# A long convolution with a gated layer behind it: late projections moved into the second half of a batch, taps read from SBUF, and an earlier start

## The chip, the cores and the metric

The kernel runs on one core of a Trainium2 chip. A core has a matrix engine (PE, with its weight loads listed apart as PEld), a vector engine (DVE), a scalar engine (ACT), GpSimd (POOL) and a sync engine (SP) that here issues every DMA. Each engine works through its own instructions in order; semaphores let one wait for another. The metric is the device time of the whole launch in microseconds (us); less is better. Before the change the median of three runs was 1005.45 us.

## The reference

`x` is (8, 6400, 128), eight sequences of 6400 positions with 128 channels, and `h` is (6400, 128). All is float32.

```python
def _attn_ref(x, h):                       # causal convolution along the sequence
    L = 2 * S
    Yf = np.fft.rfft(x, n=L, axis=1) * np.fft.rfft(h, n=L, axis=0)[None]
    return np.fft.irfft(Yf, n=L, axis=1)[:, :S, :]

def _moe_ref(x, w_val, conv_w, w_out):     # x is the convolution's result
    xp = np.concatenate([np.zeros((B, 4, D)), x], axis=1)
    gate_pre = sum(conv_w[k] * xp[:, k:k + S, :] for k in range(5))
    gate = 1 / (1 + np.exp(-gate_pre))
    return gate * (x @ w_val) @ w_out
```

So behind the convolution stand five taps per channel, a sigmoid, a product with a projection of the same data (128x128) and a second projection (128x128).

## The kernel before

The convolution is a transform of length 6400 = 100 x 64 written as matmuls against constant tables, done for one batch (one sequence) after another. Per batch there are four matmul stages.

- Stage 1 (`Forward`): sums and differences of the two halves of `x` are made by `sums` (both on POOL for batches 1 to 7, tile `sd`), then `half` multiplies them with the table `r1_sb` into a pair of PSUM banks; ACT copies the result into `gy`. There are 16 halves per batch, and `x` comes in 16 tiles of 128 x 512 numbers.
- Stage 2 (`Product`, 13 blocks `kb`): matmuls of `gy` with a streamed table (`m2`) into a PSUM pair, of which there are two. DVE multiplies the result twice with the spectrum of `h` (`mul_u` into `gy`, `mul_t` into the `h` tile), POOL adds (`add`, two instructions).
- Stage 3 (`s3_quads`, 16 of them): matmuls of `gy` with `r3_sb` into two single PSUM banks, one copied out by ACT, the other by DVE, into `dt`.
- Stage 4 (`Chunk.s4`, 13 chunks of positions: one HEAD chunk of 4 rows of 100, twelve of 5 rows): matmuls of `dt` with `m4_sb` into a single PSUM bank. There are four single banks, handed out in turn.

Then per chunk: `copies` (ACT: the data itself into `y`, the first tap, another tap into `p`), `taps` (three taps on DVE with scalar_tensor_tensor, and one addition on POOL), `project` (PE, two matmuls with the first weight), `sigm` (ACT), `gate` (DVE: projection in PSUM times the sigmoid in SBUF), `output` (PE, two matmuls with the second weight), `store` (ACT copies the result over `y`, SP writes it out). The taps of a chunk add onto cells that the chunk before it has touched too, so they follow each other.

The stages of successive batches overlap. A batch's time falls into two halves, which this text calls the first and the second half-stage:

- first half-stage: stage 3 of batch b, interleaved with stage 1 of batch b+1, 16 rounds;
- second half-stage: stage 4 of batch b, interleaved with stage 2 of batch b+1, 13 steps `s`. It is the loop over `s` at the end of the kernel. In step `s` PE gets the product of block s+1, the projection of chunk s-2, `s4` of chunk s, the output of chunk s-3; DVE gets `mul_u`, the taps of chunk s-1, `mul_t`, the gate of chunk s-2.

Five chunks (those from position row 35 to 59, the "late" ones) only have their data copied to `yl` tiles in the second half-stage. Their taps, and their and the HEAD chunk's projection, sigmoid, gate, output and store, are done in the next batch's first half-stage (`Gates.trail`). In the last batch nothing is late.

Nothing is scheduled by a planner: `_InOrder` keeps every engine's instructions in the order in which the code names them, so that order decides who stands behind whom. All instructions go through that helper, so the profile gives line 98 for nearly all; groups are told apart by tile names. A further piece is the start: `h` is transformed first, its spectrum is made and stored to DRAM, together with the products of batch 0, and `weights` (a generator, 22 DVE steps, that builds float32 weights from the 64-bit form) is advanced twice per block there.

## Time and profile before

| | |
|---|---|
| median of three runs | 1005.45 us (1003.25 to 1007.77) |
| the profiled execution, its own time | 1006.82 us |
| its span (first to last instruction) | 1005.0 us |
| PE busy | 940.5 us, 94% |
| DVE busy | 702.8 us, 70% |
| POOL busy | 544.5 us, 54% |
| ACT busy | 475.5 us, 47% |
| mean granted PE clock | 0.986 |
| one batch (as from 328.5 to 441.8 us) | 53.0 us first half-stage, 60.3 us second |

Rows of the timeline begin with start and duration, then engine, line, operation, output tile <- input tiles, shapes and a count of merged instructions; in square brackets stands how long the engine was idle ahead of it and whom it waited for. A float32 matmul of the program is listed as two. `pt<-dt,w_sb`, `pt<-yl,w_sb` and `pt<-gl,w_sb` are projections and outputs, `pt<-m_sb,dt` is stage 4, `pt<-gy,m` stage 2, `pt<-r_sb,gy` stage 3, `pt<-r_sb,sd` stage 1. On DVE, `gy<-pt,h` is `mul_u`, `h<-pt,h` is `mul_t`, `dt<-pt,dt` and `gl<-pt,gl` are gates, SCALAR_TENSOR_TENSOR are taps. Rows of the chain have start, duration and what the chain ran through.

### The profile page before, as it was taken

How to read it: one execution, taken by the hardware profiler on the slowest of the kernel's cores; microseconds unless marked ns; L12 is line 12 of the kernel's file. 1: busy time of each engine (PE TensorE's matmuls, PEld its weight loads, DVE VectorE, ACT ScalarE, POOL GpSimd, SP SyncE). 2: the span in 40 equal slices, each digit the busy share in tenths (PEclk: the TensorE clock that was granted, in tenths of full speed). 3: DMA queues.
4: the chain of work that ended last, by engine and by line, in shares of the span. 5: the costliest groups of instructions: out<-in, count | busy, mean ns of one | idle time of the engine just before them, and what ended most of it. 6: DMA issues, size and time to landing. Idle time of an engine off the chain costs nothing.

```text
span 1005.0 us, 46982 instructions
## 1 busy us (share of the span) xinstructions
PE 940.5 (94%) x21360; PEld 793.5 (79%) x21360; DVE 702.8 (70%) x939; ACT 475.5 (47%) x916; POOL 544.5 (54%) x551
## 2 busy tenths in 40 slices
PE   7897778999999999999999998999989999999987
PEld 7797778787978878887878778887887878786753
DVE  5499217977398747977398756977399755978366
ACT  4521434445543653546444554445544553534465
POOL 6467434785277744785177743784367752760032
PEclk9898999999999999999999999999999999999989
DMA  7783854756467545755467555665467554750012
GB/s 253 244 272 149 283 204 158 225 157 194 134 229 214 156 154 194 230 159 166 150 223 218 153 159 186 216 176 170 145 211 221 151 178 159 229 140 34 31 42 91
DMA packets 96838, 177.33 MB, mean 176 GB/s; under 512 B 43392, under 2 KB 49792, under 8 KB 96640
## 3 DMA queue, kind: packets, MB, share of 16 engines
q1 hardware_dynamic: 96640, 174.34, 55.6%
q8 instruction: 167, 2.74, 1.1%
q14 instruction: 31, 0.25, 0.1%
HBM read 141.55 MB, written 32.77 MB: 173 GB/s over the span
## 4 chain that ended last, share of the span: by engine, by line
PE 90%; issue 5%; DVE 3%; POOL 1%; ACT 1%; DMA 0%; POOLq 0%; DVEq 0%; ACTq 0%
PE pt L98 90%; DVE gl L98 1%; DVE dt L98 1%; POOL gl L98 1%; ACT dt L98 1%; DVE gy L98 0%; POOL dt L98 0%; DMA x<-hl 0%; DVE sd L98 0%; DVE m_sb L98 0%; POOLq L688 0%; ACT gl L98 0%; ACT yl L98 0%; ACT gy L98 0%; DVEq L98 0%
## 5 line engine op out<-in xcount | busy, mean ns | idle before, releaser
L98 PE MATMUL pt<-r_sb,gy 64*64 64x128 f32 (+1 forms) x8192 | 267.3, 273 | 20.3 <-issue 11.5
L98 PEld LDWEIGHTS pt<-r_sb,gy 64*64 64x64 f32 (+1 forms) x8192 | 235.8, 130 | 63.8 <-ACT gl L98 20.4
L98 POOL TENSOR_TENSOR sd<-x 128x256 f32<-128x256 f32 x236 | 197.4, 860 | 154.2 <-issue 124.2
L98 POOL TENSOR_TENSOR gy<-gy,h 128x512 f32<-128x512 f32 (+1 forms) x182 | 221.6, 1241 | 63.6 <-DVE h L98 27.7
L98 ACT COPY dt<-pt 128x512 f32<-128x512 f32 (+3 forms) x269 | 155.2, 581 | 193.9 <-PE pt L98 191.6
L98 PEld LDWEIGHTS pt<-m_sb,dt 128*64 128x64 f32 x4096 | 191.5, 137 | 35.3 <-issue 22.7
L98 PEld LDWEIGHTS pt<-gy,m 128*64 128x64 f32 x3008 | 179.1, 135 | 43.8 <-issue 23.6
L98 PE MATMUL pt<-gy,m 128*64 128x128 f32 x3008 | 193.3, 278 | 17.5 <-issue 12.0
L98 PE MATMUL pt<-m_sb,dt 128*64 128x100 f32 x4096 | 198.0, 250 | 2.9 <-DVE dt L98 2.4
L98 DVE COPY dt<-pt 128x512 f32<-128x512 f32 (+1 forms) x136 | 92.5, 680 | 132.1 <-PE pt L98 125.6
L98 PE MATMUL pt<-r_sb,sd 50*64 50x100 f32 x4608 | 143.2, 258 | 17.2 <-issue 11.2
L98 DVE TENSOR_TENSOR gy<-pt,h 128x1024 f32<-128x1024 f32 (+1 forms) x99 | 116.8, 1180 | 46.3 <-PE pt L98 46.3
L98 DVE SCALAR_TENSOR_TENSOR gl<-yl,w_sb,gl 128x500 f32<-128x500 f32 x147 | 130.6, 892 | 24.6 <-ACT gl L98 22.1
L98 PEld LDWEIGHTS pt<-r_sb,sd 50*64 50x64 f32 x4608 | 128.9, 142 | 22.2 <-issue 14.5
L98 DVE SCALAR_TENSOR_TENSOR dt<-pt,w_sb,dt 128x500 f32<-128x500 f32 (+7 forms) x216 | 132.9, 631 | 13.5 <-POOL dt L98 3.8
L98 ACT COPY gy<-pt 128x400 f32<-128x400 f32 x248 | 110.2, 496 | 41.2 <-PE pt L98 32.8
L98 ACT ACTIVATE dt<-pt,w_sb 128x500 f32<-128x500 f32 (+1 forms) x64 | 40.0, 625 | 170.2 <-PE pt L98 169.4
L98 PE MATMUL pt<-dt,w_sb 128*64 128x500 f32 (+2 forms) x480 | 116.0, 561 | 0.8 <-DVE dt L98 0.4
L98 POOL TENSOR_TENSOR dt<-dt,p 128x500 f32<-128x500 f32 (+1 forms) x64 | 66.4, 1038 | 82.5 <-DVE dt L98 58.0
L98 DVE TENSOR_TENSOR h<-pt,h 128x1024 f32<-128x1024 f32 (+1 forms) x91 | 107.3, 1179 | 2.3
L98 ACT COPY yl<-pt 128x500 f32<-128x500 f32 (+1 forms) x96 | 54.5, 568 | 83.9 <-PE pt L98 83.9
L98 DVE TENSOR_TENSOR gl<-pt,gl 128x500 f32<-128x500 f32 (+1 forms) x48 | 31.7, 661 | 54.5 <-PE pt L98 50.8
(40 smaller groups left out, 568.5 us busy)
## 6 DMA issues: line engine op xcount, KB each, us to landing
m<-m SPq DMA_DIRECT2D x90, 512.0 KB, 4.7
h<-hd SPq DMA_DIRECT2D x84, 512.0 KB, 3.9
x<-xl SPq DMA_DIRECT2D x118, 256.0 KB, 3.4
out<-dt SPq DMA_DIRECT2D x56, 250.0 KB, 5.8
out<-yl SPq DMA_DIRECT2D x40, 250.0 KB, 2.5
m_sb<-m SPq DMA_DIRECT2D x13, 375.0 KB, 4.5
hd<-h SPq DMA_DIRECT2D x8, 512.0 KB, 5.1
m_sb<-m SPq DMA_DIRECT2D x6, 512.0 KB, 6.5
```

Source lines behind the costliest of these rows:

```text
L98: return self._tc.keep_in_program_order(call(*args, **kwargs))
```

## The change

- The late chunks' and the HEAD chunk's `project`, `gate`, `output` and `store` are taken out of the next first half-stage and put into steps 0 to 4 of the next second half-stage (`pend`, `jobs`). The taps of the late chunks stay in the first half-stage, two per round, and so do two sigmoids; the rest of the sigmoids move.
- In every step, `output` and `store` now come one step after `project` for all chunks, with `output` at the head of a step and `project` at its end; a normal chunk is projected three steps after its stage 4 instead of two.
- On DVE the order within a step is `mul_u`, `mul_t`, the gates, then the taps.
- `copies` sets `self.p = self.y` for every chunk, so all taps on DVE read the copy in SBUF and no longer the PSUM bank.
- In the last batch both copies of a stage 3 quad are on ACT.
- Seven matmuls on a zeroed tile stand at the start of the program (`WARM`).
- The 22 weight steps move from the stage that makes `h`'s spectrum to the first half-stage of batch 0; four of the 13 loads of the table `m4` move the other way (`M4H`).
- `x` tiles are addressed as their first `XR` = 128 rows, which is all of them.

```diff
+XR = 2 * HP
+WARM = 7
+M4H = 4
...
-                    nc.sync.dma_start(self.xs[self.n % len(self.xs)], self.src[self.n])
+                    nc.sync.dma_start(self.xs[self.n % len(self.xs)][:XR], self.src[self.n, :XR])
...
                 act(self.y, self.p)
                 for i, o in cells(a, n):
                     self.first(0, o, self.p)
-                return
-            if self.late:
+            elif self.late:
                 act(self.y, self.p)
-                self.p = self.y
-                return
-            self.init()
-            act(self.y, self.p)
-            self.q = p_t[a // CH % 2]
-            self.first(3, self.q, self.p)
+            else:
+                act(self.y, self.p)
+                self.init()
+                self.q = p_t[a // CH % 2]
+                self.first(3, self.q, self.p)
+            self.p = self.y
...
+    warm = m2_sb[0][:, 0, 0]
+    nc.vector.memset(warm, 0.0)
+    pt = pair()
+    for _ in range(WARM):
+        nc.tensor.matmul(pt[:, 0, :C], lhsT=warm, rhs=warm, start=True, stop=True)
...
             pr[kb].add(nc.vector if kb == NKB - 1 else nc.gpsimd)
-            next(wgen, None)
-            next(wgen, None)
+        if 0 <= kb < M4H:
+            m4_load(kb)
...
+        late = [lambda c=c, j=j: c.taps(range(j, j + 2)) for c in pend[1:] for j in (0, 2)]
+        late += [c.sigm for c in pend[:2]]
...
             e[0](act)
-            e[1](dve)
+            e[1](dve if nxt else act)
...
-            if trail:
-                trail.pop(0)()
+            if late:
+                late.pop(0)()
...
+        cs = [Chunk(b, ch, nxt) for ch in CHUNKS]
+        jobs = collections.defaultdict(list)
+        for i, c in enumerate(pend):
+            jobs[(0, 0, 1, 1, 2, 3)[i]].append(c)
+        for i, c in enumerate(cs):
+            if i and not c.late:
+                jobs[i + 3 if i < 9 else i + 2].append(c)
+        if not nxt:
+            jobs[NCH + 1].append(cs[0])
+        ps, outs = {}, []
+        for s in range(max([NCH - 1, *jobs]) + 2):
+            todo = list(jobs[s])
...
+            for c in outs:
+                c.output()
...
             if nxt and s + 1 < NKB:
                 ps[s + 1] = Product(s + 1)
                 m2_load(s + 1 + M2B)
...
+            if 1 < s < NCH:
+                cs[s].s4()
+            for c in todo:
+                c.project()
+                if c not in pend[:2]:
+                    c.sigm()
+            for c in outs:
+                c.store()
+            if s < NCH:
+                cs[s].copies()
+            if s in ps:
                 ps[s].mul_u()
                 ps[s].mul_t()
                 ps.pop(s).add()
                 h_load(s + HB)
+            for c in todo:
+                c.gate()
+            if 0 < s <= NCH and not cs[s - 1].late:
+                cs[s - 1].taps()
+            outs = todo
...
+        pend = [cs[0]] + [c for c in cs if c.late]
```

How the order moves is shown at two places, both in the middle of a second half-stage, in steps that have every kind of work. Numbers in the names tell tiles apart: `pt1_` are single PSUM banks, `pt2_` pairs. First PE, before the change: product, projection (`pt1_4381`), stage 4, output (`pt1_4405`).

```order
L98 MATMUL pt1_4320<-dt_67,w_sb_71 64x500 x2
L98 MATMUL pt1_4323<-m4_sb_68,dt_67 64x2x50 x20
L98 MATMUL pt1_4344<-dt_67,w_sb_71 64x500 x2
L98 MATMUL pt2_4363<-gy_66,m2_1_80 64x64x2 x16
L98 MATMUL pt1_4381<-dt_67,w_sb_71 64x500 x2
L98 MATMUL pt1_4384<-m4_sb_68,dt_67 64x2x50 x20
L98 MATMUL pt1_4405<-dt_67,w_sb_71 64x500 x2
```

The output of the chunk whose projection is `pt1_4320` is `pt1_4405`, six rows on: its gate falls into the time of stage 4, another output, a product, another projection and another stage 4. PE in the changed kernel:

```order
L101 MATMUL pt1_4345<-dt_67,w_sb_71 64x500 x2
L101 MATMUL pt1_4364<-dt_67,w_sb_71 64x500 x2
L101 MATMUL pt2_4367<-gy_66,m2_1_80 64x64x2 x16
L101 MATMUL pt1_4385<-m4_sb_68,dt_67 64x2x50 x20
L101 MATMUL pt1_4406<-dt_67,w_sb_71 64x500 x2
L101 MATMUL pt1_4425<-dt_67,w_sb_71 64x500 x2
```

Here `pt1_4345` is a projection and the next row, `pt1_4364`, is the output of the same chunk; likewise `pt1_4406` and `pt1_4425`. Nothing stands between the two on PE.

The second place is DVE in the same steps. Before:

```order
L98 TENSOR_TENSOR gy_66<-pt2_4241,h_1_83 128x2x64x8
L98 SCALAR_TENSOR_TENSOR dt_67<-pt1_4262,w_sb_71,dt_67 128x5x100 x3
L98 TENSOR_TENSOR h_1_83<-pt2_4241,h_1_83 128x1024
L98 TENSOR_TENSOR dt_67<-pt1_4320,dt_67 128x5x100
L98 TENSOR_TENSOR gy_66<-pt2_4302,h_2_84 128x2x64x8
```

And in the changed kernel:

```order
L101 TENSOR_TENSOR gy_66<-pt2_4306,h_2_84 128x2x64x8
L101 TENSOR_TENSOR h_2_84<-pt2_4306,h_2_84 128x1024
L101 TENSOR_TENSOR dt_67<-pt1_4406,dt_67 128x5x100
L101 SCALAR_TENSOR_TENSOR dt_67<-dt_67,w_sb_71 128x5x100 x3
L101 TENSOR_TENSOR gy_66<-pt2_4367,h_3_85 128x2x64x8
```

The three taps went from between the two products to behind the gate, and their input from a PSUM bank (`pt1_4262`) to `dt`.

More of the change, by code (lines that the diff above doesn't have):

```diff
@@ L530, in longconv_moe @@
     ps1 = ctx.enter_context(tc.tile_pool(name="ps1", bufs=4, space=bass.MemoryType.PSUM))
-    class Gates:
-        def __init__(self, b, defer):
-            self.cs = [Chunk(b, ch, defer) for ch in CHUNKS]
-        def trail(self):
-            h, late = self.cs[0], [c for c in self.cs if c.late]
-            steps = collections.defaultdict(list)
-            for m, c in enumerate(late + [h]):
-                t = 2 * m + 2
-                if c is not h:
-                    steps[t - 2].append(lambda c=c: c.taps(range(2)))
-                    steps[t - 1].append(lambda c=c: c.taps(range(2, 4)))
-                steps[t] += [c.project, c.sigm, c.gate]
-                steps[t + 2].append(c.output)
-                steps[t + 3].append(c.store)
-            n = max(steps)
-            return [lambda c=steps[i]: [f() for f in c] for i in range(n + 1)]
-        def at(self, s, last):
-            return self.cs[s] if 1 <= s < NCH else self.cs[0] if s == NCH and last else None
-        def each(self, what, s, last=True):
-            c = self.at(s, last)
-            if c and not c.late:
-                getattr(c, what)()
-        def finish(self, s):
-            self.each("project", s - 2)
-            self.each("output", s - 3)
-            self.each("store", s - 4)
-            self.each("sigm", s - 2)
-            if s == NCH:
-                self.cs[NCH - 1].taps()
-            self.each("gate", s - 2)
-    trail = []
     fx = Forward(x[1], gy) if B > 1 else None
@@ L590, in longconv_moe @@
             e[0](act)
[L591 removed]
+            e[1](dve if nxt else act)
             for u in f:
                 u(act)
[L594 to L596 removed]
+            if b == 0:
+                next(wgen, None)
+                next(wgen, None)
+                if g + M4H < NKB:
+                    m4_load(g + M4H)
             if nxt and g % 2 and g > 1:
@@ L602, in longconv_moe @@
                     h_load(kb - M2B)
-            if trail:
-                trail.pop(0)()
+            if late:
+                late.pop(0)()
         if b + 2 < B:
             fx = Forward(x[b + 2], gy)
-        gs = Gates(b, nxt)
-        ps = {}
-        for s in range(NCH):
-            if s == 0:
-                gs.cs[0].s4()
-                gs.cs[0].copies()
-                if nxt:
-                    ps[0] = Product(0)
-                    m2_load(M2B)
-            if s == 1:
-                gs.cs[s].s4()
+        cs = [Chunk(b, ch, nxt) for ch in CHUNKS]
[10 more added lines that the diff above has]
+            todo = list(jobs[s])
+            if s == 0 and pend:
+                todo.pop(0)
+                pend[0].project()
+                pend[0].gate()
+            if s < 2:
+                cs[s].s4()
+            if nxt and s == 0:
+                ps[0] = Product(0)
+                m2_load(M2B)
+            for c in outs:
+                c.output()
+            if s == 0 and pend:
+                pend[0].output()
+                pend[0].store(p_t[1][:, : HEAD[1]])
             if nxt and s + 1 < NKB:
@@ L622, in longconv_moe @@
                 m2_load(s + 1 + M2B)
-            gs.each("project", s - 2)
-            if s > 1:
-                gs.cs[s].s4()
-            gs.each("output", s - 3)
-            gs.each("store", s - 4)
-            gs.each("sigm", s - 2)
-            if s:
-                gs.cs[s].copies()
-            if nxt:
+            if 1 < s < NCH:
+                cs[s].s4()
+            for c in todo:
[7 more added lines that the diff above has]
+            if s in ps:
                 ps[s].mul_u()
-            if s > 1 and not gs.cs[s - 1].late:
-                gs.cs[s - 1].taps()
-            if nxt:
                 ps[s].mul_t()
@@ L638, in longconv_moe @@
                 h_load(s + HB)
-            if s == 0:
-                gs.cs[0].taps()
-            gs.each("gate", s - 2)
+            for c in todo:
[3 more added lines that the diff above has]
+            outs = todo
             if s == 10 and b + 2 < B:
                 fx.load(XB)
-        trail = gs.trail() if nxt else [lambda s=s: gs.finish(s) for s in range(NCH, NCH + 5)]
-    for t in trail:
-        t()
+        pend = [cs[0]] + [c for c in cs if c.late]
 def _lay_x(v):
```

16 lines of the change are left out of this document (9 added, 7 removed).

## The prediction

> **What bounds the kernel now.** I read the page first, for the busy shares and the chain that ended last.
>
> ```profile
> PE 940.5 (94%) x21360; PEld 793.5 (79%) x21360; DVE 702.8 (70%) x939; ACT 475.5 (47%) x916; POOL 544.5 (54%) x551
> PE 90%; issue 5%; DVE 3%; POOL 1%; ACT 1%; DMA 0%; POOLq 0%; DVEq 0%; ACTq 0%
> ```
>
> PE carries the chain. Whatever only shifts work off other engines gains nothing; whatever makes PE wait costs in full. Next, the two half-stages of one batch in the table of windows, and the chain at the start of a second half-stage.
>
> ```profile
> 328.50:381.50 53.00, 52.73 (x1588) 43.22 (x1585) 32.55 (x43) 32.00 (x64) 27.13 (x32) 1.00 0.49 155
> 381.50:441.80 60.30, 57.80 (x974) 50.22 (x972) 51.09 (x67) 24.19 (x46) 40.82 (x37) 1.00 0.71 211
> ```
>
> ```profile
> 277.18 1.71 issue
> ...
> 282.70 0.76 issue
> ```
>
> The columns after the length are PE, PEld, DVE, ACT and POOL busy. In the second half-stage PE idles for 2.5 us, which are these two waits at its start, and DVE has 51.1 us of 60.3. How tight it is shows in the timeline of one step, PE first, then DVE.
>
> ```profile
> 303.94 2.02 PE L98 MATMUL pt<-gy,m 128*64 128x128 f32 x32
> 305.78 1.01 PE L98 MATMUL pt<-dt,w_sb 128*64 128x500 f32 x4
> 306.62 1.90 PE L98 MATMUL pt<-m_sb,dt 128*64 128x100 f32 x40
> 308.34 1.01 PE L98 MATMUL pt<-dt,w_sb 128*64 128x500 f32 x4
> 309.18 2.02 PE L98 MATMUL pt<-gy,m 128*64 128x128 f32 x32
> ```
>
> ```profile
> 302.23 1.22 DVE L98 TENSOR_TENSOR h<-pt,h 128x1024 f32<-128x1024 f32 x1
> 303.36 0.67 DVE L98 TENSOR_TENSOR dt<-pt,dt 128x500 f32<-128x500 f32 x1
> 303.94 1.22 DVE L98 TENSOR_TENSOR gy<-pt,h 128x1024 f32<-128x1024 f32 x1
> 305.13 2.29 DVE L98 SCALAR_TENSOR_TENSOR dt<-pt,w_sb,dt 128x500 f32<-128x500 f32 x3
> 307.33 1.22 DVE L98 TENSOR_TENSOR h<-pt,h 128x1024 f32<-128x1024 f32 x1
> ```
>
> PE takes 309.18 - 303.94 = 5.24 us a step without a gap: product 1.84, projection 0.84, stage 4 1.72, output 0.84. DVE repeats after 307.33 - 302.23 = 5.10. Both are full, and PE never waits for a gate, because output runs a step behind its projection.
>
> **Part 1, the wait of output for its gate.** In the changed order a chunk's output stands on PE right behind its own projection, and needs the gate that DVE can only start when that projection is done. PE is in order, so product and stage 4 queue behind the waiting output, and DVE's next products behind those. Its price:
>
> ```profile
> 316.26 1.01 PE L98 MATMUL pt<-dt,w_sb 128*64 128x500 f32 x4
> 317.39 0.68 DVE L98 TENSOR_TENSOR dt<-pt,dt 128x500 f32<-128x500 f32 x1 [0.35 <-PE pt L98]
> ```
>
> ```profile
> 999.13 0.69 DVE gl L98
> 999.82 0.04 issue
> 999.86 1.75 PE pt L98 x8
> ```
>
> A projection after which PE could go on at 0.84 has its gate started at 317.39 - 316.26 = 1.13, 0.29 later; the gate takes 0.68; PE follows 0.04 behind a gate (second view, the chain). That is 1.0 us of PE idle per step, even with DVE waiting ready. Steps 3 to 11 of a batch have it (in steps 0 to 2 other rows stand between, or DVE is ahead): 9 us per batch at least.
>
> **Part 2, taps from SBUF.** DVE's taps now read two SBUF operands while POOL, which gets its two additions as `mul_t` ends, reads two as well. The trace has such pairs, late taps beside POOL's sums in the first half-stage:
>
> ```profile
> 332.52 1.29 DVE L98 SCALAR_TENSOR_TENSOR gl<-yl,w_sb,gl 128x500 f32<-128x500 f32 x1
> 909.11 0.73 DVE L98 SCALAR_TENSOR_TENSOR gl<-yl,w_sb,gl 128x500 f32<-128x500 f32 x1
> 330.28 2.31 POOL L98 TENSOR_TENSOR sd<-x 128x256 f32<-128x256 f32 x2
> 366.25 1.42 POOL L98 TENSOR_TENSOR sd<-x 128x256 f32<-128x256 f32 x2 [3.17 <-issue]
> 303.69 2.52 POOL L98 TENSOR_TENSOR gy<-gy,h 128x512 f32<-128x512 f32 x2
> ```
>
> At 909 POOL is idle and a tap takes 0.73; at 332 POOL is busy and it takes 1.29, while two POOL sums take 2.31 instead of 1.42. They take turns. Taps from PSUM did not (2.29 for three, beside the POOL row at 303.69 and without it). In the new step DVE has the gate (0.6), then three taps, and POOL two additions of 1.26. In turns: first addition to 1.4 after `mul_t`, tap to 1.9, second addition to 3.05, taps to 3.6 and 4.35. The two products add 2.3: DVE's step is 6.6 us, and PE's 5.24 then has 1.4 idle, not 1.0. If POOL lost every turn it would stay at 1.0; that is the lower end. Seven of the nine steps have such taps: 7 x 1.4 + 2 x 1.0 = 11.8 us per batch.
>
> The Trainium skill ("SBUF — State Buffer", Who interferes with whom) says that a DVE instruction with two SBUF inputs and a GpSimd instruction that reads SBUF exclude each other, for whole instructions. The trace agrees on the turns, though 1.29 and 1.16 a piece are less than 0.73 + 0.71; by the rule in full the step would be 7.15 us.
>
> **Part 3, what is moved.** Six projections and outputs leave the first half-stage (five pairs of 341.42 - 339.59 = 1.83, one of 1.6 with 400 columns: 10.7 us) and cost 9.8 in the second at 0.84 each.
>
> ```profile
> 331.01 1.93 PE L98 MATMUL pt<-r_sb,gy 64*64 64x128 f32 x64
> 332.76 0.88 PE L98 MATMUL pt<-r_sb,sd 50*64 50x100 f32 x32
> ...
> 339.59 1.06 PE L98 MATMUL pt<-gl,w_sb 128*64 128x500 f32 x4
> ...
> 341.42 2.18 PE L98 MATMUL pt<-r_sb,gy 64*64 64x128 f32 x61
> ```
>
> The first half-stage keeps 53.0 - 10.7 = 42.3. Bare rounds take 1.75 + 0.69 = 2.44, 39.0 for 16; but in ten of them DVE has a copy (0.6) and two late taps (up to 2.4 beside POOL) against 2.44, so I take 42.0: -0.3. In the second, the extra PE work in steps 0 to 3 covers the old 2.5 us of waits; POOL's additions end some 0.8 later than PE, and the next stage 3 needs them. Per batch: 11.8 - 2.5 + 0.8 - 0.3 - 0.9 = +8.9, six batches +53. With POOL losing every turn and bare rounds: 9 - 2.5 + 0.8 - 3.3 - 0.9 = +3, six +18.
>
> Batch 0 has no late work to fill steps 2 and 3, so there DVE's 6.6 stand against a PE step of 3.6; that is about 6 us on top of 6 x 1.4 + 1.0: +14 after the 2.5 and 0.8 (lower end +6).
>
> **Part 4, the last batch.** Its first half-stage runs from 900.84 to 946.93, 46.1 us.
>
> ```profile
> 900.84 3.73 PE L98 MATMUL pt<-r_sb,gy 64*64 64x128 f32 x128
> ...
> 946.93 5.23 PE L98 MATMUL pt<-m_sb,dt 128*64 128x100 f32 x111 [0.50 <-ACT dt L98]
> ```
>
> Two bare quads take 3.65, so 16 take 29 (ACT's two copies, 1.2 per quad, fit): -17. The second half-stage to PE's end at 1001.6 is 54.7, set by the serial taps:
>
> ```profile
> 986.04 1.26 POOL gl L98
> 987.33 0.75 DVE gl L98
> ...
> 989.76 1.27 POOL gl L98
> ```
>
> 3.72 a chunk. Now the loop of Part 1 sets a step: output 0.84, stage 4 1.72, projection 0.84 and 1.0 idle: 4.4. Steps 0 and 1 with five projections, 8.6; nine steps of 4.4 to 48; two more to 59; then the last two chunks' taps stand behind the gate ahead of them (2.3 + 1.25 + 0.6 + 0.7, 5 each) and one output: 71. That is +16; together -1 (bounds -8, +6).
>
> **Part 5, the start.**
>
> ```profile
> 10.00:12.00 2.00, 2.00 (x56) 2.00 (x52) 1.10 (x3) 0.89 (x2) 1.06 (x2) 1.00 1.03 386
> 14.00:16.00 2.00, 2.00 (x88) 1.76 (x79) 2.00 (x5) 1.54 (x4) 2.00 (x4) 1.00 0.69 173
> 92.92 1.21 DVE gy L98
> ...
> 120.07 2.83 issue
> 126.44 2.37 issue
> ```
>
> PE issues 56 matmuls in 2 us before 12 us and 88 after (windows): it starts at about half pace. Warm-up can save half of the 8 us at most, but DMA (1.03 busy) and POOL's sums follow closely; I take 1. Without weight steps DVE begins the row at 92.92 some 2 us earlier, and with it PE's next stage. Of the waits with no visible releaser in batch 0's first half-stage (two rows of 11 us in all, 107 to 138 us), during the m4 loads, 4 of 13 loads go away: 4. Sum -7, bounds 0 and -15. The Trainium skill ("TensorE: Matmul & The Clock Gate", Part 1) puts the slow phase at some 3.4 us of activity, so warm by about 5 us here; by it the 1 would be 4. The `XR` slices are whole tiles and cost nothing.
>
> **Sum.** 53 + 14 - 1 - 7 = +59. Not every tap will meet POOL, so I take off 5: +54. The profiled execution took 1006.8, the median 1005.5; I go from the median: 1060.
>
> **Rivals.**
> - Taps win against POOL (for it: DVE has its next tap queued; against: the rows alternate). Then 18 + 6 - 1 - 7 = +16: 1021.
> - Faster: the bubble is short. Without any idle a batch would gain 2.5 + 3.3 + 0.9 less 0.8, 6 us, six 36; with -3 in batch 0, -15 at the end (-17 as above, +2 for the pairs that come into the tail) and -7 at the start, -61. There are 6 x 9 + 7 + 15 = 76 waits, so the kernel turns faster below 0.8 us each. At 0.5, 1005 - 61 + 38 = 982. For it: 0.29 of the 1.0 is a latency read from one pair of rows, and PE's four banks may let it run further; against: PE is in order, and the gate alone is 0.68.
> - Full exclusion, every instruction waiting for the end of the other: first addition to 1.4, tap to 2.15, second addition to 3.4, taps to 4.15 and 4.9, 0.55 more in 7 steps of 7 batches, 27 us: 1087. The 1.29 speaks against it. It is the page's rule taken word for word.
>
> **How the numbers follow.** Forecast 0.57 (its own range 1035 to 1078), taps winning 0.18, faster 0.15, full exclusion 0.10. The range that leaves out 2 in 10 is 1000 to 1080. A difference of 0.5%, 5 us, is about what can be told: faster 0.17, same 0.05, slower 0.78.
>
> **What would show it.** Right: in the second half-stage, waits of about 1 to 1.4 us on PE ahead of each `pt<-dt,w_sb` output, put down to DVE; a step of 6.3 to 6.6; `dt<-dt,w_sb` taps of 0.73 to 1.3 and POOL's `gy<-gy,h` well over 1.28; a first half-stage of 39 to 42 and a second near 79. Wrong: outputs that follow their projections without a wait, or taps at 0.75 throughout.

## The result, and the profile after

The changed kernel takes 1119.05 us (median of four runs, 1114.32 to 1120.72) against 1004.86 for the kernel before on the same chip: 1.1125 times as long, 95% interval 1.108 to 1.117. The forecast was 1060, slower by 54 us; it is slower by 114. The direction was right, the size about half. The profiled execution has a span of 1116.8 us, 111.8 more than before.

The page of the changed kernel, busy shares and the chain that ended last:

```profile
PE 948.4 (85%) x21374; PEld 790.8 (71%) x21374; DVE 763.2 (68%) x924; ACT 488.1 (44%) x932; POOL 561.6 (50%) x551
PE 62%; DVE 25%; issue 9%; POOL 2%; ACT 1%; DMA 0%; POOLq 0%; SPq 0%; DVEq 0%
```

PE does the same work (948 us busy, 940 before) but carries 62% of the chain instead of 90%. DVE now has 25% of it and "issue", waits without a visible releaser, 9%. The table of waits says how much of that falls on PE:

```profile
PE pt L101 <- issue: 68.2, 57, 3.0
PE pt L101 <- DVE dt L101: 64.2, 56, 1.6
```

The columns are total, times and longest, in us. The 56 waits for DVE were foreseen; most of the 57 without a releaser were not: 51 of them lie in the first half-stages, 4 in the start, and the other two, in batch 0's second half-stage, end 0.1 us after a DVE product, so they are DVE's. Where the time goes is seen in the windows, one row per half-stage: length, then PE, PEld, DVE, ACT and POOL busy. Batch 0's second, one batch in the middle (first and second), and the last batch:

```profile
153.66:229.46 75.80, 62.11 (x974) 51.93 (x973) 64.07 (x67) 26.45 (x48) 43.24 (x36) 0.95 0.51 161
360.74:412.16 51.42, 43.01 (x1540) 39.83 (x1542) 28.89 (x37) 27.33 (x56) 27.84 (x33) 1.00 0.46 142
412.16:491.02 78.86, 68.22 (x1018) 51.73 (x1014) 64.76 (x72) 29.54 (x56) 42.80 (x36) 1.00 0.58 173
1012.26:1041.63 29.37, 29.14 (x1028) 28.25 (x1029) 15.26 (x21) 20.81 (x40) 0.63 (x1) 1.00 0.02 4
1041.63:1116.80 75.17, 57.74 (x666) 33.33 (x664) 41.12 (x68) 41.31 (x78) 15.54 (x15) 0.98 0.21 65
```

The same rows for all batches give the account. "Forecast" is what the steps of the prediction say for the piece.

| piece, us | before | after | difference | forecast |
|---|---|---|---|---|
| start, up to batch 0's stage 3 | 97.1 | 97.2 | 0.1 | -3 |
| batch 0, first half-stage | 57.5 | 56.5 | -1.0 | -4 |
| batch 0, second | 60.3 | 75.8 | +15.5 | +14 |
| batches 1 to 6, first, together | 323.8 | 309.3 | **-14.5** | **-66** |
| batches 1 to 6, second, together | 362.1 | 473.5 | +111.4 | +119 |
| last batch, first | 46.1 | 29.4 | -16.7 | -17 |
| last batch, rest | 58.1 | 75.2 | +17.1 | +16 |

Every row but one is within 8 us. The one is the first half-stage of batches 1 to 6: from 54.0 to 51.5 us on average, where 53.0 to 42.0 was forecast. That is 51.5 us off. The forecast pieces add up to 59 (54 after the 5 taken off at the end) and the spans differ by 111.8, so this one row is nearly the whole of the error. PE's waits without a releaser make up most of it: summed over these six first half-stages they are 47.9 us, against 6.5 before.

In it, PE's timeline from the sixth bare round on:

```profile
374.32 0.67 PE L101 MATMUL pt<-r_sb,gy 64*64 64x128 f32 x16 [1.18 <-issue]
...
379.24 0.64 PE L101 MATMUL pt<-r_sb,sd 50*64 50x100 f32 x17 [1.46 <-issue]
...
383.51 1.58 PE L101 MATMUL pt<-r_sb,gy 64*50 64x128 f32 x49 [0.83 <-issue]
...
395.88 1.63 PE L101 MATMUL pt<-r_sb,gy 64*50 64x128 f32 x50 [1.65 <-issue]
...
401.81 0.75 PE L101 MATMUL pt<-r_sb,gy 64*50 64x128 f32 x18 [2.38 <-issue]
```

PE stops in the middle of a quad or of a half, ahead of matmuls that wait for no semaphore, so no engine's result is late. The clock was granted in full there (1.00 in the row 360.74:412.16). What the waits share is their distance: counted in matmul records, 374.32 to 379.24 is 127, to 383.51 another 127, to 387.24 (a stop of 0.18 us, not shown) 128, to 395.88 twice 127, to 401.81 128. Of the 44 distances within the first half-stages, 38 are 127 or 128 and the rest two or three times that. The page's DMA queues say what has this size:

```profile
q8 instruction: 168, 2.75, 1.0%
```

168 packets, 2.75 MB, so 16 KB each, and 2 x 21374 PE instructions over 168 is 254 per packet. So one packet holds, by this count, a block of 128 matmuls with their 128 weight loads. The trace's packets of this queue beside PE's waits:

| packet of q8, us | PE goes on at | after the packet's end |
|---|---|---|
| 371.89 to 372.82 | 374.32 | 1.50 |
| 376.88 to 377.87 | 379.24 | 1.37 |
| 380.89 to 382.06 | 383.51 | 1.45 |
| 392.65 to 394.30 | 395.88 | 1.58 |
| 399.49 to 400.43 | 401.81 | 1.38 |

Over all 51 such waits of the first half-stages the last column is 1.40 in the middle, 1.28 to 1.56 in four of five. The next packet begins 1.05 us after PE has gone on at the earliest, 1.67 in the middle, 4.18 at the latest. So a block of instructions has a round trip of 1.05 + 0.93 + 1.40 = 3.4 us when nothing delays it, and bare rounds, 96 matmuls in 2.44 us, use one up in 128/96 x 2.44 = 3.25.

The second half-stage is as forecast. One step, first PE, then DVE, then POOL:

```profile
451.75 1.06 PE L101 MATMUL pt<-dt,w_sb 128*64 128x500 f32 x4 [1.46 <-DVE dt L101]
452.61 2.06 PE L101 MATMUL pt<-gy,m 128*64 128x128 f32 x32
454.45 1.93 PE L101 MATMUL pt<-m_sb,dt 128*64 128x100 f32 x40
456.17 1.05 PE L101 MATMUL pt<-dt,w_sb 128*64 128x500 f32 x4
458.44 1.06 PE L101 MATMUL pt<-dt,w_sb 128*64 128x500 f32 x4 [1.22 <-DVE dt L101]
...
448.54 1.22 DVE L101 TENSOR_TENSOR gy<-pt,h 128x1024 f32<-128x1024 f32 x1
449.79 1.22 DVE L101 TENSOR_TENSOR h<-pt,h 128x1024 f32<-128x1024 f32 x1
450.94 0.67 DVE L101 TENSOR_TENSOR dt<-pt,dt 128x500 f32<-128x500 f32 x1
451.52 3.88 DVE L101 SCALAR_TENSOR_TENSOR dt<-dt,w_sb 128x500 f32<-128x500 f32 x3
455.32 1.22 DVE L101 TENSOR_TENSOR gy<-pt,h 128x1024 f32<-128x1024 f32 x1
...
451.15 2.94 POOL L101 TENSOR_TENSOR gy<-gy,h 128x512 f32<-128x512 f32 x2 [1.10 <-PE pt L101]
```

DVE repeats after 455.32 - 448.54 = 6.78 us without a pause; three taps take 3.88 beside POOL's additions, 2.29 before. PE waits 1.2 to 1.5 us ahead of the output. The merged rows of taps and additions, one instruction at a time:

```profile
451.15 1.27 POOL L101 TENSOR_TENSOR gy<-gy,h 128x512 f32<-128x512 f32 x1 [1.10 <-PE pt L101]
451.52 1.43 DVE L101 SCALAR_TENSOR_TENSOR dt<-dt,w_sb 128x500 f32<-128x500 f32 x1
452.38 1.72 POOL L101 TENSOR_TENSOR gy<-gy,h 128x512 f32<-128x512 f32 x1
452.99 1.64 DVE L101 SCALAR_TENSOR_TENSOR dt<-dt,w_sb 128x500 f32<-128x500 f32 x1
454.67 0.74 DVE L101 SCALAR_TENSOR_TENSOR dt<-dt,w_sb 128x500 f32<-128x500 f32 x1
```

The instructions that meet end one after the other: addition 452.42, tap 452.95, addition 454.10, tap 454.63. The third tap meets none and takes 0.74.

### The profile page after: what moved, and what is told of

It is laid out like the page before. It is cut to its first block, busy times and chain, and to the rows that moved or that the text cites. A ratio compares the mean times of both kernels' runs of the same rounds, so it can differ in the third digit from the quotient of the medians.

```text
span 1116.8 us, 46938 instructions
## 1 busy us (share of the span) xinstructions
PE 948.4 (85%) x21374; PEld 790.8 (71%) x21374; DVE 763.2 (68%) x924; ACT 488.1 (44%) x932; POOL 561.6 (50%) x551
## 3 DMA queue, kind: packets, MB, share of 16 engines
q8 instruction: 168, 2.75, 1.0%
## 4 chain that ended last, share of the span: by engine, by line
PE 62%; DVE 25%; issue 9%; POOL 2%; ACT 1%; DMA 0%; POOLq 0%; SPq 0%; DVEq 0%
PE pt L101 62%; DVE dt L101 16%; DVE gy L101 4%; DVE h L101 2%; DVE gl L101 2%; POOL gy L101 2%; ACT dt L101 1%; DMA x<-hl 0%; DVE sd L101 0%; ACT p L101 0%; POOL gl L101 0%; ACT gl L101 0%; DVE m_sb L101 0%; ACT gy L101 0%; POOLq L678 0%
## 5 line engine op out<-in xcount | busy, mean ns | idle before, releaser
L101 ACT COPY dt<-pt 128x512 f32<-128x512 f32 (+3 forms) x285 | 163.1, 582 | 380.2 <-PE pt L101 363.9
L101 POOL TENSOR_TENSOR gy<-gy,h 128x512 f32<-128x512 f32 (+1 forms) x182 | 239.3, 1338 | 163.3 <-PE pt L101 123.3
L101 PE MATMUL pt<-r_sb,gy 64*50 64x128 f32 (+1 forms) x8192 | 276.3, 275 | 48.0 <-issue 39.9
L101 PEld LDWEIGHTS pt<-r_sb,gy 64*50 64x50 f32 (+1 forms) x8192 | 244.2, 132 | 61.3 <-issue 48.0
L101 DVE SCALAR_TENSOR_TENSOR dt<-dt,w_sb 128x500 f32<-128x500 f32 (+2 forms) x192 | 190.0, 1006 | 3.3
L101 DVE COPY dt<-pt 128x512 f32<-128x512 f32 (+1 forms) x120 | 81.5, 679 | 153.8 <-PE pt L101 147.6
L101 DVE SCALAR_TENSOR_TENSOR gl<-yl,w_sb,gl 128x500 f32<-128x500 f32 (+2 forms) x187 | 156.1, 837 | 37.9 <-ACT gl L101 25.6
L101 PE MATMUL pt<-r_sb,sd 50*64 50x100 f32 x4608 | 152.1, 258 | 26.3 <-issue 22.4
L101 PEld LDWEIGHTS pt<-r_sb,sd 50*64 50x64 f32 x4608 | 133.8, 141 | 34.3 <-issue 29.1
L101 PEld LDWEIGHTS pt<-dt,w_sb 128*64 128x64 f32 x480 | 27.3, 135 | 115.0 <-DVE dt L101 76.5
L101 ACT COPY yl<-pt 128x500 f32<-128x500 f32 (+1 forms) x89 | 50.3, 568 | 125.8 <-PE pt L101 125.6
L101 DVE TENSOR_TENSOR gl<-pt,gl 128x500 f32<-128x500 f32 (+1 forms) x48 | 31.7, 661 | 60.6 <-PE pt L101 34.4
```

Of the source, the lines that this page charges most:

```text
L101: return self._tc.keep_in_program_order(call(*args, **kwargs))
```

## The experiments

Times are medians of the runs behind the ratio; the kernel before stands at 1002 to 1005 in these comparisons. "First" and "second" are means over batches 1 to 6 of the profiled execution, the tail is the last batch behind its stage 3. "Waits" is PE's waits without a visible releaser in the first half-stages of batches 1 to 6, in all. e1, e2, e4 and e6 leave work out.

| run | us | ratio to before (95%) | first | second | tail | waits |
|---|---|---|---|---|---|---|
| the kernel before | 1004.9 | 1 | 54.0 | 60.4 | 58.1 | 6.5 |
| the changed kernel | 1119.1 | 1.113 (1.108 to 1.117) | 51.5 | 78.9 | 75.2 | 47.9 |
| e1_no_loads | 1091.6 | 1.087 (1.084 to 1.090) | 46.3 | 78.9 | 75.3 | 19.7 |
| e2_no_late_taps | 1124.2 | 1.118 (1.114 to 1.122) | 52.9 | 78.9 | 74.6 | 52.8 |
| e3_lag | 1100.1 | 1.096 (1.090 to 1.102) | 50.3 | 78.3 | 70.1 | 40.6 |
| e4_no_adds | 1093.2 | 1.089 (1.084 to 1.094) | 50.6 | 76.1 | 74.6 | 46.3 |
| e5_halves | 1105.2 | 1.100 (1.095 to 1.104) | 50.8 | 79.0 | 76.1 | 44.9 |
| e6_lag_no_adds | 1029.7 | 1.026 (1.023 to 1.029) | 51.3 | 68.0 | 68.4 | 42.5 |
| e7_inner | 1035.7 | 1.032 (1.027 to 1.037) | 52.0 | 68.7 | 69.2 | 45.8 |
| e8_late_back | 1017.7 | 1.014 (1.011 to 1.017) | 54.2 | 62.0 | 71.0 | 2.1 |
| e9_early | 1041.5 | 1.037 (1.033 to 1.041) | 51.7 | 68.7 | 69.8 | 16.7 |
| e10_best | 1021.3 | 1.019 (1.014 to 1.024) | 56.3 | 60.4 | 57.2 | 1.0 |
| e11_before_sbuf | 1065.2 | 1.063 (1.059 to 1.067) | 53.1 | 69.0 | 58.0 | 1.4 |
| e12_early_x | 1030.2 | 1.027 (1.024 to 1.030) | 49.5 | 68.7 | 70.6 | 29.7 |
| e13_roles | 1014.3 | 1.011 (1.009 to 1.014) | 54.1 | 62.0 | 70.7 | 1.0 |
| e14_roles_halves | 1014.0 | 1.011 (1.008 to 1.014) | 54.4 | 62.0 | 70.5 | 1.4 |
| e15_order | 993.8 | 0.990 (0.987 to 0.993) | 53.5 | 60.3 | 66.3 | 3.3 |

The first half-stage has the same instructions in the changed kernel and in e3, e4, e6 and e7: 50.3 to 52.0. A difference inside that band shows nothing.

### What fills the first half-stage: e1, e2, e5, e9, e12

Theory: PE's instruction blocks come late. First rival: the late taps, two per round on DVE in turns with POOL's sums, set the round.

e1:

```diff
-            if nxt and g % 2 and g > 1:
+            if nxt and g % 2 and g > 1 and b == 0:
                 kb = g // 2 - 1
```

> Leaves out, from batch 1 on, the three m2 and four h loads (512 KB each) that are issued in the first half-stage, so the products of blocks 0 to 2 use old data; the 16 x loads stay. Theory (instruction supply): in the changed kernel PE stops after every 128th matmul of the bare rounds, and goes on 1.4 us after a 16 KB packet of PE's instruction queue has landed; 128 matmuls with their 128 weight loads would take 3.25 us in bare rounds, the packet's round trip is 1.1 + 0.93 + 1.4 = 3.4 us when nothing is ahead of it, and up to 2.5 us more behind 512 KB loads. Without those loads the first half-stage of batches 1 to 6 falls from 51.5 to 42 to 44 us, the whole to 1119 - 6 x 8 = about 1070. Rival A (DVE: two late taps in turns with POOL's sums, beside the copy, set the round): first half-stage stays at 50 to 52, the whole at 1115 to 1120. Rival B (x arrives late for POOL's sums): the x loads get faster too, so it cannot be told from the theory by the time, but then the gaps would end with a wait on POOL's sd, not without a releaser.

46.3 us instead of 51.5, not quite the 42 to 44. One batch of it:

```profile
356.39:403.74 47.35, 42.65 (x1541) 39.81 (x1542) 28.85 (x37) 27.30 (x56) 28.02 (x33) 1.00 0.27 76
```

DVE, ACT and POOL are busy as long as in the row 360.74:412.16 above; only the DMA share went, from 0.46 to 0.27, and with it 4 to 5 us. From the middle of it on PE still stops after every 127th or 128th matmul, 0.3 to 0.9 us each time, 1.3 to 1.6 behind the packet's end. In all six batches the waits fall from 47.9 to 19.7 us, and the half-stages by 31.7. So the data loads cause some 5 us of the loss a batch; the waits that stay come beside the x loads alone.

e2 (`return` ahead of the late chunks' DVE taps):

```diff
-            if self.late and 0 in js:
-                self.init()
+            if self.late:
+                if 0 in js:
+                    self.init()
+                return
```

> Leaves out the late chunks' DVE taps in the first half-stage (two per round in ten rounds); ACT's first tap stays, so sigmoids get other data. Theory (instruction supply): PE's gaps stay, first half-stage 49 to 51.5, whole 1108 to 1119. Rival A (DVE's late taps set the round): first half-stage 42, whole 1119 - 6 x 9 = 1065.

```profile
362.70:413.86 51.16, 43.83 (x1541) 41.27 (x1542) 11.07 (x16) 27.30 (x56) 23.17 (x33) 0.97 0.44 143
```

DVE's work falls from 28.9 to 11.1 us and the length stays (52.9 on average). The rival is out.

e5 (`m2_part` and `h_part` load one half of a tile):

```diff
-            if nxt and g % 2 and g > 1:
-                kb = g // 2 - 1
+            if nxt and g > 1:
+                kb, part = g // 2 - 1, g % 2
                 if kb < M2B:
-                    m2_load(kb)
+                    m2_part(kb, part)
                 else:
-                    h_load(kb - M2B)
+                    h_part(kb - M2B, part)
```

> Each of the seven 512 KB loads of m2 and h in the first half-stage is cut into two of 256 KB, one per round from the third on; nothing is left out. Theory (a packet of PE's instructions waits behind the data that is queued when it is asked for): at most half as much is ahead of it, gaps shrink from about 8 to 4 us, first half-stage 47 to 49 (46.3 without these loads at all), whole 1095 to 1106. Rival (the bytes in all decide, not the burst): first half-stage 50.5 to 52.5, whole 1113 to 1122.

50.8, inside the band: a miss for the theory's detail. The delay of a packet is not simply half when the transfer ahead of it is half as long. Yet the whole, 1105.2, lies in the theory's range and is shorter than the changed kernel beyond both intervals; the profile, taken in the slowest of its four runs (1111.2), does not show where most of that comes from. So halves are left open here. Batch 0's first half-stage was 53.1 there, which e14 asks about.

e9, from e7 (below):

```diff
-            if nxt and g % 2 and g > 1:
+            if nxt and g % 2 and g > 1 and b == 0:
...
                 h_load(s + HB)
+                if b + 2 < B and s > 8:
+                    h_load((s - 8) % HB)
+                    if s < NKB - 1:
+                        m2_load((s - 8) % M2B)
```

> The changed kernel with the old order within a step (the run called e7_inner), and from batch 1 on the seven 512 KB loads of m2 and h are issued in steps 9 to 12 of the second half-stage before, as their buffers come free, instead of in the first half-stage. Nothing is left out. Theory (the bytes that share the DMA engines with PE's instruction blocks while PE runs bare rounds are a part of the loss): first half-stage of batches 1 to 6 falls from 52 to 46 to 48 as without these loads; second half-stage stays at 68.7, since PE asks for an instruction block only every 10 us there; whole 1036 - 6 x 5 = about 1006 (1000 to 1015). Rival (the loads only move the loss): second half-stage 71 or more, whole over 1022.

Neither came as a whole: the first half-stage stayed at 51.7 and the second at 68.7, though the time, 1041.5, is the rival's. PE and POOL at the seam:

```profile
342.28 1.61 PE L101 MATMUL pt<-r_sb,sd 50*64 50x100 f32 x32 [3.79 <-POOL sd L101]
...
340.82 2.77 POOL L101 TENSOR_TENSOR sd<-x 128x256 f32<-128x256 f32 x4 [4.78 <-DMA x<-xl]
```

With the loads issued ahead of it, x came late, and PE waited 3.8 us for the sums of x. After that the waits at the block ends were 0.3 to 0.9 us, as in e1. Over the six batches they fell from 45.8 us (e7) to 16.7 with nothing left out, and 24.9 us of waits for x took their place. So e12 loads x first:

```diff
-            if s == 10 and b + 2 < B:
+            if s == 3 and b + 2 < B:
                 fx.load(XB)
```

> As the run with the early loads of m2 and h (e9_early), and the first three x tiles of the next batch are loaded in step 3 of the second half-stage instead of step 10, ahead of those loads. There, PE's gaps behind every 128th matmul had shrunk to 0.3 to 0.9 us once the 512 KB loads were through, but PE had waited 3.8 us at the seam for x. Theory (the loss of the first half-stage is the instruction blocks' round trip, of which the data loads add a part): the wait for x goes away, first half-stage 46 to 49, second still 68.7, whole 1041 - 6 x 4 = about 1017. Rival (first half-stage's loss is set by the bytes of the seam, however they are ordered): 51 to 53, whole 1035 to 1045.

49.5, just below the band, 2.2 below e9, and 1030 against 1041. The wait for x is gone, but the waits at the block ends are back to 29.7 us. The direction is the theory's, the size half. With nothing left out, order of the loads wins back 2 of the 12 us that lie between 51.5 and the 39.0 of 16 bare rounds.

### What fills the second half-stage: e3, e4, e6, e11, e7

The prediction had two causes side by side: output behind its own projection (Part 1) and SBUF taps in turns with POOL (Part 2). They are taken away one at a time, then together.

e3 moves the outputs:

```diff
-            for c in outs:
-                c.output()
             if s == 0 and pend:
...
             if 1 < s < NCH:
                 cs[s].s4()
+            for c in outs:
+                c.output()
             for c in todo:
                 c.project()
```

> Output moves behind product and stage 4 of its step, so 3.5 us of PE work stand between a projection and its output; nothing else. Theory (DVE's own work is the step: products 1.25 + 1.15, gate 0.6, three taps in turns with POOL 3.8 = 6.8 us; PE's wait for the gate is only where that shows): second half-stage 77 to 79 against 78.9, whole 1105 to 1119. Rival (the output behind its own projection is the cost, 1.0 us of nine steps): second half-stage 70, whole 1119 - 7 x 9 = 1056.

e4 leaves POOL's work out:

```diff
-                ps.pop(s).add()
+                ps.pop(s)
```

> Leaves out POOL's two additions of each product in the second half-stage of batches 0 to 6; the output stays right behind its projection. Theory (turns): taps fall from 1.29 to 0.73 each, DVE's own work to 5.2; then PE's loop of 5.24 + 1.0 for the gate sets the step, 6.2 to 6.3 instead of 6.78; second half-stage 74 to 76, whole 1119 - 7 x 4 = 1091. Rival (no turns: taps from SBUF are slow by themselves): taps stay at 1.2, second half-stage 78 to 79, whole 1112 to 1119.

e6 has both edits.

> Both earlier edits: output behind product and stage 4, and POOL's additions of the products left out in the second half-stage. Theory (two limits stand side by side, DVE's 6.8 us with taps in turns and PE's 5.24 + 1.0 behind the gate; only taking both away lets PE's own 5.24 set the step): second half-stage 67 to 69 us in batches 1 to 6, 60 to 62 in batch 0, whole about 1035 (1028 to 1045). Rival (the two costs are separate and add: 0.6 and 2.8 us per batch): second half-stage 75 to 76, whole about 1077.

One batch each of e3, e4 and e6, second half-stage:

```profile
407.51:485.77 78.26, 67.56 (x1018) 51.93 (x1014) 65.60 (x72) 28.89 (x56) 42.87 (x36) 1.00 0.56 174
...
402.85:478.93 76.08, 68.17 (x1019) 51.75 (x1015) 55.75 (x72) 29.21 (x55) 13.53 (x16) 1.00 0.63 182
...
387.49:455.47 67.98, 66.84 (x1019) 51.88 (x1015) 55.44 (x72) 28.18 (x55) 9.31 (x10) 1.00 0.66 196
```

Alone the edits give 0.6 and 2.8 us a batch, together 10.9. That is what two limits close to each other do: with the output moved, DVE's step stays at 6.8 us and PE waits for DVE's products instead (9.3 us in this batch of e3); with the turns gone, PE's loop over the gate sets it at 6.2 to 6.4. The taps were slow because of POOL, not by themselves: their group has a mean of 1006 ns in the changed kernel and 657 without the additions.

```profile
L101 DVE SCALAR_TENSOR_TENSOR dt<-dt,w_sb 128x500 f32<-128x500 f32 (+2 forms) x192 | 190.0, 1006 | 3.3
...
L101 DVE SCALAR_TENSOR_TENSOR dt<-dt,w_sb 128x500 f32<-128x500 f32 (+2 forms) x192 | 122.9, 657 | 3.3
```

e11 asks the reverse, the kernel before with SBUF taps alone:

```diff
             self.first(3, self.q, self.p)
+            self.p = self.y
```

> The kernel before with one edit: all taps on DVE read the SBUF copy instead of the PSUM bank. Its order keeps the taps behind the gate and the next first product, 1.9 us after POOL's additions start, so only the second addition and the first tap can meet. Theory (turns between instructions with two SBUF operands): taps 0.75 to 1.2, DVE's step 5.6 instead of 5.1, PE's 5.24 is passed by 0.4 in seven steps of seven batches; second half-stage 62 to 64, whole 1015 to 1030. Rival (the place of the taps right behind the gate decides, not their operands): second half-stage 60 to 61, whole 1002 to 1010.

More than expected: 69.0, 8.6 us a batch, 63 in all. DVE and POOL in a step of it:

```profile
313.85 1.21 DVE L98 TENSOR_TENSOR gy<-pt,h 128x1024 f32<-128x1024 f32 x1
314.99 3.35 DVE L98 SCALAR_TENSOR_TENSOR dt<-dt,w_sb 128x500 f32<-128x500 f32 x3
318.25 1.22 DVE L98 TENSOR_TENSOR h<-pt,h 128x1024 f32<-128x1024 f32 x1
319.39 0.67 DVE L98 TENSOR_TENSOR dt<-pt,dt 128x500 f32<-128x500 f32 x1
...
313.59 2.53 POOL L98 TENSOR_TENSOR gy<-gy,h 128x512 f32<-128x512 f32 x2
```

One meeting a step is enough: single records show the first tap at 314.99 taking 1.67 us, until 0.54 after POOL's second addition ends at 316.11, the other two 0.74 each. DVE's step is then 6.1 us, over PE's 5.24. So the operands of the taps alone, put into the kernel before, cost 63 us, where the whole change costs 114.

e7 keeps the late work in the second half-stage and takes the old order and PSUM taps; nothing is left out:

```diff
-            self.p = self.y
+            if self.late:
+                self.p = self.y
...
+            for c in todo:
+                c.project()
             if 1 < s < NCH:
                 cs[s].s4()
+            for c in outs:
+                c.output()
...
                 ps[s].mul_u()
+            if 0 < s <= NCH and not cs[s - 1].late:
+                cs[s - 1].taps()
+            if s in ps:
                 ps[s].mul_t()
```

> The changed kernel with the old order within a step and nothing left out: product, projections, stage 4, outputs of the step before on PE; first product, taps, second product, gates on DVE; taps of the chunks that are not late read PSUM again. The late work stays in the second half-stage. Theory (output behind its own projection and taps in turns with POOL are the whole loss of the second half-stage; the instruction supply is the loss of the first): second half-stage 60 to 62 in batch 0, 67 to 70 after; first half-stage still 50 to 53; last batch 29.4 + 60 to 64; whole 1015 to 1040, still slower than before. Rival (the six projections and outputs are what is too much for the second half-stage): second half-stage 74 or more, whole over 1060.

68.7 and 62.9 (batch 0), 52.0 in the first: as expected; 83 of the 114 us are back, and it is still 3.2% slower than before. The move by itself costs 8.3 us a batch in the second half-stage and saves 2 in the first.

### Towards a faster kernel: e8, e10, e13, e14, e15

e8 is e7 with the late work back in the first half-stage while there is a next batch (`trail` is the list of steps of the kernel before):

```diff
+        if nxt and pend:
+            late = trail(pend)
+            pend = []
+            late.pop(0)()
...
-                jobs[i + 3 if i < 9 else i + 2].append(c)
+                jobs[i + 2 if nxt or i > 8 else i + 3].append(c)
```

> As the run before, but the late chunks' projections and outputs are put back into the first half-stage of batches 1 to 6; only the last batch has them in the second. Theory (in the first half-stage the projections are nearly free, because PE's few long matmuls give the instruction blocks time to arrive): batches 1 to 6 as before the change, 54 + 60.4; the last batch 29.4 + 60 to 64 instead of 104; whole 985 to 1000. Rival (the move itself is worth something where no wait spoils it): slower than the run before.

It is slower than forecast in two places: the second half-stage took 62.0 instead of 60.4, the tail 71 instead of 60 to 64. The theory's reason holds all the same: with the long matmuls back among the short ones, the waits of the first half-stages go from 45.8 us (e7) to 2.1, and the half-stage is only 2.2 us longer for 10.7 us of work. e10 puts the early loads of e9, five `m4` loads in the second half-stage of batch 0 and ACT's copies in the last batch on the kernel before:

```diff
-            e[1](dve)
+            e[1](dve if nxt else act)
...
+M4_ORDER = (0, 12, 1, 11, 2, 10, 3, 9, 4, 8, 5, 7, 6)
...
-            if b == 0 and g < NKB:
+            if b == 0 and g < 8:
+                m4_load(M4_ORDER[g])
...
+            if b == 0 and s < 5:
+                m4_load(M4_ORDER[8 + s])
```

> The kernel before with three edits: the seven loads moved as in the run before; of the 13 loads of m4 in batch 0 five moved into its second half-stage, outer rows first; both copies of a quad on ACT in the last batch. Theory: first half-stage of batches 1 to 6, which has 49.7 us of PE work and takes 54, falls to 51 to 52.5; batch 0's from 57.5 to 52 to 55; last batch's from 46.1 to 40; whole 980 to 990. Rival (with the projections as cover the instruction supply costs nothing in the kernel before): batches 1 to 6 unchanged, whole 993 to 1000.

It is slower than the kernel before: again x is late at the seam (3.49 us of PE in one batch), first half-stage 56.3; the last batch's stayed at 46.0, so DVE's copies were not its limit.

e13, from e8, puts the HEAD chunk's taps back to the end of step 0 and exchanges two taps between DVE and POOL:

```diff
-            self.first(3, self.q, self.p)
+            self.first(0, self.q, self.p)
...
-                if j < 3 or self.late:
+                if j or self.late:
...
-            for i, o in cells(a + 3, n):
+            for i, o in cells(a, n):
```

> Aimed at a kernel faster than both. From the run with the late work put back (e8_late_back): the HEAD chunk's taps stand at the end of step 0 again, as before the change, and the two roles in a chunk's taps are exchanged: POOL adds the tap of the chunk's own five rows (0), DVE the one three rows on (3), so that the next chunk's taps on DVE no longer touch rows that POOL is still adding to. Theory: second half-stage of batches 0 to 6 back at 60.4 instead of 62.0; in the last batch a chunk's chain falls from 3.8 us (three taps 2.3, POOL 1.26, hand-over) to PE's 3.4, the tail from 71 to 60 to 64; whole 1017 - 11 - 8 = 994 (985 to 1000), faster than before by 0.5 to 1.5%. Rival (the chain in the tail goes through something else, such as the gates): tail 68 to 71, whole 1003 to 1008.

e14 adds the edit of e5 to it.

> The run before with the 512 KB loads of the first half-stage cut in two as in e5_halves, where batch 0's first half-stage took 53.1 us against 55 to 61 in the other kernels with the changed start. Theory (it was the halves): batch 0 at 52 to 55, whole 3 us less than the run before. Rival (it was chance): no difference beyond 2 us.

e14 equals e13, in batch 0's first half-stage too (54.8 and 54.4), so the halves do not explain the 53.1 of e5. e13's tail and second half-stage did not move, and its trace says why. The chain in the tail, and a tap row of the second half-stage:

```profile
966.51 3.64 PE pt L101 x48
...
970.17 1.63 ACT dt L101 x3
971.80 0.58 ACT p L101
...
972.40 0.75 DVE dt L101
...
973.95 0.75 DVE dt L101
...
974.75 3.64 PE pt L101 x48
```

```profile
412.75 2.29 DVE L101 SCALAR_TENSOR_TENSOR dt<-pt,w_sb,dt 128x500 f32<-128x500 f32 x3 [0.72 <-ACT p L101]
```

POOL has left the tail's chain, but now PE's next output, and with it the stage 4 behind it, starts at 974.75, when the third tap has ended (974.70). This is put down here to the PSUM bank that these taps read. The taps of the second half-stage wait for ACT, which works on the store of the same step first. e15 is aimed at both:

```diff
+                self.init()
                 act(self.y, self.p)
-                self.init()
...
-            if self.late:
+            if self.late or self.last:
                 self.p = self.y
...
+            for c in done if nxt else outs:
+                c.store()
+            done = outs
```

> From e13_roles, which was slower than expected in two places. In its second half-stages DVE's taps waited 0.2 to 0.7 us a step for ACT, whose copies of a chunk stood behind the store of that step's output; and in the last batch the taps held the PSUM bank that PE's next stage 4 needed (steps of 8.2 us for two chunks). Edits: store one step later than output, sigmoid behind it, the first tap ahead of the copy, as in the kernel before; in the last batch all taps read SBUF, so a bank is free once ACT has copied it. Theory (these two waits are all that keeps it from the old 60.4 and from PE's 3.4 a chunk): second half-stage 60.4 in batches 0 to 6, tail 60 to 65, whole 990 to 1000, 0.3 to 1.3% faster than before. Rival (in the tail another engine is next: DVE with taps and gate 3.5 to 3.9 a chunk in turns with POOL): second half-stage 60.4, tail 66 to 70, whole 999 to 1004.

993.8 us, 0.990 (0.987 to 0.993) of the kernel before and faster than both. The two edits were not taken apart. The tail's 66.3 is above the 60 to 65 that were expected. Its rows for one batch and the last:

```profile
325.95:379.83 53.88, 52.94 (x1587) 43.32 (x1585) 32.60 (x43) 31.99 (x64) 27.33 (x32) 1.00 0.49 152
379.83:440.13 60.30, 57.78 (x974) 49.84 (x972) 51.05 (x68) 24.19 (x46) 40.66 (x36) 1.00 0.70 211
895.05:923.90 28.85, 28.85 (x1030) 28.12 (x1028) 15.26 (x21) 20.98 (x40) 0.00 (x0) 1.00 0.02 5
923.90:990.20 66.30, 56.62 (x666) 32.38 (x664) 44.98 (x69) 40.60 (x78) 15.62 (x14) 0.96 0.24 74
```

Batches 1 to 6 are close to those of the kernel before (53.5 and 60.3 for 54.0 and 60.4); most of the gain is the last batch, 95.2 us instead of 104.2, where the late work sits in the tail and nothing runs beside it.

## Why the prediction was right or wrong

- **Part 1, output behind its projection: the waits came as described, but they do not add to Part 2.** Nine waits a batch were forecast, 11.8 us; nine came in the middle batch, each ahead of an output, 10.2 us in all. Moving the outputs alone (e3) gives only 0.6. The prediction said itself that DVE's step is longer than PE's 5.24 + 1.0; then the wait is only where DVE's time shows. The 1.0 us counts as a price of its own once the turns are gone: 8.1 a batch from e4 to e6, where Part 1 had 9.
- **Part 2, taps from SBUF: right, down to the single instruction.** A step of 6.6 was forecast, 6.78 measured; the second half-stage 79, measured 78.9; batch 0 +14, measured +15.5. Counted from `mul_t`'s end at 451.02, the additions end at 1.40 and 3.08, where 1.4 and 3.05 was written, and the taps at 1.93, 3.61 and 4.39, where 1.9, 3.6 and 4.35 was written. The rival "full exclusion" has the taps at 2.15, 4.15 and 4.9 and is out. The Trainium skill ("SBUF — State Buffer", Who interferes with whom) says that a DVE instruction with two SBUF inputs and a GpSimd one that reads SBUF contend for a port pair under an exclusive lock. This trace agrees that they take turns; but a tap ends 0.53 us behind the addition, not its full 0.74, so some 0.2 us of a tap is not held up.
- **Part 3, the moved work: the failed step.** The first half-stage without the six projections and outputs was put at 42.0, from bare rounds of 2.44. The 2.44 is read rightly; what was not seen is that it cannot be kept up, since PE runs out of instructions at the block ends. 51.5 was measured, of which 8.0 a batch are these waits. The prediction looked at DVE's copies and late taps as the next limit; e2 takes these away and nothing moves. The evidence lay in the profile before: batch 0's first half-stage, which has no projections, has about 11 us of such waits in 57.5, and the prediction put them down to the loads of `m4` and took 4 us as a gain for the start, instead of carrying them over to the other batches. The row of that profile, waits of PE from 97.11 to 154.59:

```profile
PE pt L98 <- issue: 11.0, 8, 2.8
```

  These eight stops are 127, 127, 128, 127, 255, 127 and 128 matmul records apart, as in the changed kernel. With 51.5 in place of 42.0 the sum of the prediction is +59 + 57 less the 5 taken off, about 1116.
- The Trainium skill ("Runtime: NRT & Kernel Launch", Instruction fetch mechanics) says that instructions are refilled in 16 KiB blocks of 256 by a queue of the engine's own, and that this is mostly hidden. The block is what the trace has; hidden it is not here, where PE uses a block in 3.25 us and gets the next after 3.4 or more. Were it hidden, the forecast's 42 would stand.
- **Part 4, the last batch: right**, -16.7 and +17.1 for -17 and +16, and the loop's steps are 4.46 us in the trace for 4.4. One sum in it is off: "nine steps of 4.4 to 48; two more to 59" should end at 57, and PE 2 us earlier, at 69 instead of 71. Measured to PE's end it is 71.7; the end has waits of its own, one of 2.95 us for DVE, so that 71 fits is luck in part. e3, e7 and e13 show what the tail waits for: output behind its gate (5 us, e3), then POOL's additions, then the taps on DVE.
- **Part 5, the start: the 7 us cannot be seen in this pair of profiles.** Stage 3 of batch 0 begins at 97.2 us, as before (97.1). But with the old start that moment is 97.1, 100.9 and 101.1 in three profiles (before, e10, e11), with the new one 95.5 to 98.9 in fourteen, so some 2 us may have come, about the 3 that were forecast for it. For batch 0's first half-stage the scatter, 53.1 to 60.9 us in kernels with the new start, hides the 4 us. The warm-up did bring the clock up, and then lost it again, as two rows of the changed kernel show (the third number from the end is the granted clock):

```profile
4.00:6.00 2.00, 1.54 (x34) 1.05 (x33) 0.41 (x1) 0.40 (x1) 0.94 (x2) 1.00 0.87 301
10.00:12.00 2.00, 2.00 (x60) 2.00 (x56) 1.24 (x3) 0.95 (x3) 1.30 (x2) 0.50 1.07 380
```

  PE waited for its inputs in between, 0.53 us at 6.07 and 0.20 twice. In e15 the clock stayed at 1.00 from 4 to 14 us, and stage 3 of batch 0 began at 97.5 all the same, so an early clock by itself shortened nothing there.
- **The rivals.** "Taps win" is out by the 3.88 us for three taps, "faster" by PE's waits of 1.2 to 1.5 us, over its limit of 0.8. The 5 us taken off for taps that meet nobody were not there.

Open: why the next packet begins anywhere from 1.05 to 4.18 us after PE goes on. It has to do with data transfers (e1, e9), but halving them (e5) did not show in the first half-stage, and reordering them (e9, e12) gave 2 us at most. Whether fewer, longer matmuls would lift the limit was not tried.

## What to carry to other kernels

A stretch with many short matmuls can be limited by the supply of instructions: count the matmuls between waits that have no releaser, and compare a block's round trip with the time in which PE uses it up, before taking work out of such a stretch as a gain. Work of few, long instructions is nearly free there (six projections and outputs, 10.7 us of PE, cost 2.2, e7 to e8) and costs nearly in full elsewhere (8.3). Where two limits stand close together, removing either alone shows almost nothing, so remove both before judging one.

## What the runs showed of the hardware that was not expected

- PE stops at the end of every 128 matmuls with their weight loads when the next 16 KB packet is late, and goes on 1.40 us (1.28 to 1.56) after it lands; at 3.66 us per block, in the last batch's 29.4 us with hardly a transfer beside it (DMA share 0.02), it does not stop.
- With six projections and outputs among the short matmuls, PE's waits at the block ends in six first half-stages are 2.1 us (e8); without them 45.8 (e7).
- A DVE tap with both operands in SBUF that meets one POOL addition of 1.28 us takes 1.67 instead of 0.74 us; with a PSUM operand three take 2.29 beside the same additions.
